# Queueing the first decodes of a fused attention and SwiGLU chain behind the gates of its items

## The chip, the cores and the metric

The kernel runs on one core of one Trainium2 chip. The metric is the time of one execution on the device in microseconds; several executions are timed and their median is given. The engines of the core are TensorE (PE; its weight loads are listed as PEld), VectorE (DVE), ScalarE (ACT), GpSimd (POOL) and SyncE (SP), whose queue issues most of the transfers. Each engine works through its own queue in order.

## The reference

Everything is float32. Attention is done twice: a packed query `p` (32 rows) reads keys and values, and the packed result serves as keys and values for the queries. The result is flattened to 4608 tokens of 512 and goes through a SwiGLU layer and a bilinear one.

```python
def _attn_ref(q, k, v, p):                       # batch 8, heads 8, seq 576, dim 64
    def sm_attn(qq, kk, vv): ...                 # softmax(scale * qq kk^T) vv
    p_packed = sm_attn(p, k, v)
    return sm_attn(q, p_packed, p_packed)

def _moe_ref(x, w_in, w_out):                    # 512 -> 2048 -> 512
    h = x @ w_in
    g = h * (1.0 / (1.0 + np.exp(-h)))
    return (g @ w_out).astype(np.float32)

def _moe2_ref(x, w1, w2, w3, w_out):             # 512 -> 1024 -> 512
    a = x @ w1
    b = x @ w2
    return (((a * b) @ w3) @ w_out).astype(np.float32)
```

## The kernel before

Matrix products keep float32 accuracy by splitting each operand into a high part (rounded to the type fp32r) and a low part, and adding three products (`mm3`, lines 97 to 100: one matmul on each of the lines 98, 99 and 100). The high part is a copy, mostly on ScalarE (line 82), the low part a subtraction on VectorE or GpSimd (line 91).

The span has two halves. Up to about 840 us an attention and SwiGLU stage runs, a loop over 256 *items* `(b, f, m)`: batch element, half of its 576 rows, one 128-wide block of the 2048 hidden columns. For an item:

- `emit_h` multiplies the block's first factor (a slot of `mq`, packed values times a block of `w_in`) with the attention weights `a2`: 6 matmuls of 288 columns into a PSUM tile `ps_h` of a pool with **two** banks;
- `emit_g` takes tanh of half of it on ScalarE (`sg`, line 874), then the gate on VectorE (`gg`, line 879), which reads `ps_h` and so frees its bank, then the high part `gh` on ScalarE and the low part `gl` on GpSimd;
- `emit_x2`, three items later, multiplies `gh` and `gl` with the second factor `wo[m]`, 12 matmuls into four banks `acc0` to `acc3` (`ps_x`).

After it comes the bilinear layer, which the change doesn't touch.

The weights arrive as 64-bit words and have to be decoded into float32. `Decode` (from line 174) does for one tile of 128x512: two conversions on ScalarE (line 82), a shift (line 190) and a mask (line 192) on VectorE, and a sum on GpSimd (line 196). For the first ones an intermediate tile `ps_dec` stands in one of the banks acc2 and acc3; once the second product of item 0 has been written out by the program they go without it, in place in SBUF. There are 32 decodes in the start: i0 to i7, o0 to o7, i8 to i15, o8 to o15 (`i`: a piece of `w_in`; `o`: one `wo[m]`, which is split as well, the low part mostly on GpSimd).

The order in which the program writes out the work of the start is the string `START`, cut by `|`: what stands ahead of the first `|` comes ahead of item 0, and each further piece comes at the end of one item, behind its `emit_g`. `L` loads a raw tile on SyncE's queue, `F` decodes one. P0, P1 are the steps of the packed attention of batch elements 0 and 1; S0, S1 those of the second attention of element 0, first and second half of its rows. `D` (`direct0`) makes a quarter's first factors for one group of heads right in the slots: two products of plain float32 (line 693; each has two matmul records) into a `ps_h` bank, then the split (lines 82 and 91) into `mq`. It has to come ahead of `P1.tail`, which copies element 1's packed values into the blocks `mbd` that the product reads. `T` (`direct`, line 704) makes the same products for both elements and stores them to DRAM; `W` stores pieces of `w_in`.

The program's order isn't the order in the queues. A planner goes through the program with a model of the engines and puts what is ready at an engine first into its queue, by order in the program where several are ready. A decode whose raw tile has landed can so stand far ahead of the item with which it is written. `tc.issue_after(ins)` takes that freedom: what is written within it goes behind `ins` in `ins`'s own queue. `hold(*names)` does so for the instructions kept in `behind`: "sg" is the tanh of the latest item and "gg" its gate. Before, this is used for later work (the decodes from item 70 on among it) and not for the F of the start. For items 0 to 15 all stores and loads of SyncE queue behind the last raw load written (`behind[DMA]`).

Of the kernel before, what the change touches and what calls it, by code (L numbers as in the profile page):

```python
# [23 lines left out]
def attention_swiglu_chain(  # L24
# [27 lines left out]
    H, D, NPK = 8, 64, 32  # L52
# [16 lines left out]

    START = (  # L70
        "P0.load P0.load_v P0.split_v0 S0.load P0.prepare L L L P1.load P1.load_v P1.prepare P1.split_v0 L L "
        "P0 P0 P0 P0 P0.tail S0 S0 P1 F L F L S1.load S0 P1 F L F L D D P1 F L F L P1 F L F L D D P1.tail F "
        "| F L F L S1 | F L S1 | F F S1 | F F T T | T T | T T | T T L | W W L | F L W W | W W | F L W W | | F L "
        "| | F L | | F T T | T T | F L | | F L | | F T T | T T | W W | L W W | F L W W | W W "
        "| F L | F L | F L | F L | F L | F L | F | S0 S1 |"
    )
# [2 lines left out]
    V, A, T, G, DMA = nc.vector, nc.scalar, nc.tensor, nc.gpsimd, nc.sync  # L79
# [22 lines left out]
    behind = {}  # L102

    def hold(*names):

        stack = ExitStack()
        for x in names:
            stack.enter_context(tc.issue_after(behind[x]))
        return stack
# [573 lines left out]
    def store_wi(i):  # L683
        g, c = divmod(i, CD)
        move(out=wi_d[g, 128 * c:128 * c + 128], in_=zi[i])

    def direct0(g, hg):

        assert all(("i", CD * g + c) in ready for c in range(CD))
        ps = ps_h.tile([128, 512], F32, tag="h", name="ps_m0")  # L690
        for c in (2 * hg, 2 * hg + 1):
            w = m_blocks(True)[:, 0, c].rearrange("p y h n -> p (y h n)")
            T.matmul(out=ps, lhsT=w, rhs=zi[CD * g + c], start=c % 2 == 0, stop=c % 2 == 1)
        dst = slots[:, 4 * g:4 * g + 4, hg]
        split(dst[:, :, 0], dst[:, :, 1], ps.rearrange("p (j f) -> p j f", j=4))
        for j in range(4):
            holds[4 * g + j] = (0, 4 * g + j)

    def direct(g, c):

        assert ("i", CD * g + c) in ready
        ps = bank("ps_m0")
        w = m_blocks(True)[:, 0, c].rearrange("p y h n -> p (y h n)")
        T.matmul(out=ps, lhsT=w, rhs=zi[CD * g + c], start=True, stop=True)
        ms = at.tile([128, 512], F32, tag="ms", name="ms", bufs=NM)
        act_copy(ms, ps)
        move(out=m01_d[g][c], in_=ms)
        if c == CD - 1:
            m_done.update([(0, g), (1, g)])
# [67 lines left out]
    def act(token):  # L777

        if token == "F":
            fill.step()  # L780
        elif token == "L":
            fill.load()
        elif token == "D":
            direct0(*todo0.pop(0))
        elif token == "T":
            direct(*todo.pop(0))
        elif token == "W":
            store_wi(to_store.pop(0))
        else:
            name, _, what = token.partition(".")  # L790
            if what:
                for u in first[name]:
                    getattr(u, what)()
            else:
                for x in runs[name]:
                    next(x)
# [3 lines left out]
    def act_on():  # L800
        for token in plan:
            if token == "|":
                return
            act(token)

    act_on()


# [345 lines left out]
    W = 384  # L1154
# [159 lines left out]
    for i, (b, f, m) in enumerate(items):  # L1314
        if i == KM:
            for eng in (DMA, A):
                behind.pop(eng, None)
        flush()
        fetch(i)
        ps = emit_h(i)  # L1320
        if i >= LAG:
            emit_x2(i - LAG)
        emit_g(i, ps)
        for y in "xyz":
            while done[y] < due(y, i):
                done[y] += 1
                next(streams[y], None)
        act_on()
        if i == prep_end:
            drain(streams["y"])  # L1330
            drain(streams["x"])
            flush()
            early = ctx.enter_context(tc.tile_pool(name="early", bufs=1, side="right"))
            load_x2(0)
            for n in range(2):
                for name in USED:
                    load_left(n, name)
                load_z34(n)
            drain(first_right_factors())
# [355 lines left out]
```

## Time and profile before

| | us |
|---|---|
| median of 3 runs | 1393.79 |
| lowest and highest of them | 1393.56, 1398.23 |
| the profiled execution | 1392.33 |
| its span, first to last instruction | 1390.4 |
| TensorE busy | 1350.9 |
| VectorE busy | 970.3 |
| ScalarE busy | 736.4 |
| GpSimd busy | 919.5 |

The profile is one execution. A wait is idle time of an engine, put down to the instruction that ended it. A VectorE or GpSimd instruction's duration contains the time in which it is held up by the other engine. TensorE's matmuls are pipelined, so their durations overlap: a matmul of 288 columns lasts some 0.3 us in the trace and the next one starts 0.13 us after it.

### The profile page before, as it was taken

The page shows a single profiled execution, that of the slowest core. Times are in us where ns is not written, and L with a number is a line of the kernel's source. Part 1 is how long each engine was busy: PE and PEld are TensorE (multiplying, and loading weights), DVE is VectorE, ACT ScalarE, POOL GpSimd, SP SyncE. Part 2 cuts the span into 40 slices and gives each one's busy share as a digit, 9 for nine tenths or more (in the row PEclk, how much of TensorE's full clock was granted, in tenths as well). Part 3 has the DMA queues.
Part 4 walks back from the last instruction along what each step waited for, and adds up shares of the span by engine and source line. Part 5 has one row for each costly group of instructions (what it writes and reads, how often), then busy time and mean ns, then how long its engine had stood idle before and what let it go on. Part 6 is the DMA issues. An engine that isn't in the chain of part 4 may idle for free. (4 is left out here: it accounts for less than half of the span.)

```text
span 1390.4 us, 26650 instructions
## 1 busy us (share of the span) xinstructions
PE 1350.9 (97%) x9197; PEld 1307.8 (94%) x9197; DVE 970.3 (70%) x1642; ACT 736.4 (53%) x1653; POOL 919.5 (66%) x874
## 2 busy tenths in 40 slices
PE   7889899999999999999999999899999999999998
PEld 5578899999999999999999999899999999999998
DVE  5997756458776578777669747885765766766665
ACT  6857566565765566665556645453334443433432
POOL 2879857766879677887677644664754756647632
PEclk9999999999999999999999999999999999999999
DMA  9698546744676443865547648657667677576751
GB/s 328 212 324 271 154 147 194 207 128 144 210 230 207 148 147 112 276 200 160 186 144 240 206 163 282 196 174 214 212 175 231 179 211 215 173 218 206 215 160 54
DMA packets 191557, 272.94 MB, mean 196 GB/s; under 512 B 18752, under 2 KB 112320, under 8 KB 191424
## 3 DMA queue, kind: packets, MB, share of 16 engines
q1 hardware_dynamic: 173168, 251.20, 58.6%
q10 hardware_dynamic: 18256, 20.06, 4.1%
q8 instruction: 73, 1.20, 0.4%
q14 instruction: 60, 0.49, 0.1%
HBM read 209.06 MB, written 62.13 MB: 195 GB/s over the span
## 5 line engine op out<-in xcount | busy, mean ns | idle before, releaser
L98 PE MATMUL ps_x<-gh,wo 128*128 128x288 f32 x1024 | 300.6, 297 | 2.7 <-DVE xs L916 2.7
L99 PE MATMUL ps_x<-gh,wo 128*128 128x288 f32 x1024 | 299.8, 295 | 0.0
L100 PE MATMUL ps_x<-gl,wo 128*128 128x288 f32 x1024 | 288.8, 297 | 0.5 <-POOL gl L91 0.4
L91 POOL TENSOR_TENSOR gl<-gg,gh 128x288 fp32r<-128x288 f32 x256 | 231.8, 908 | 80.0 <-ACT gh L82 65.3
L879 DVE SCALAR_TENSOR_TENSOR gg<-sg,ps_h 128x288 f32<-128x288 f32 x256 | 114.1, 447 | 133.1 <-ACT sg L874 81.1
L1517 DVE TENSOR_TENSOR o<-o,ps_o 128x768 f32<-128x768 f32 x137 | 130.2, 951 | 101.3 <-PE ps_o L1535 100.5
L98 PEld LDWEIGHTS ps_x<-gh,wo 128*128 128x128 f32 x1024 | 192.0, 188 | 5.6 <-DVE xs L916 2.3
L99 PEld LDWEIGHTS ps_x<-gh,wo 128*128 128x128 f32 x1024 | 192.2, 188 | 2.2 <-issue 1.4
L91 POOL TENSOR_TENSOR mq<-mr,mq 128x256 fp32r<-128x256 f32 x168 | 143.6, 855 | 72.2 <-DVE mq L86 40.7
L100 PEld LDWEIGHTS ps_x<-gl,wo 128*128 128x128 f32 x1024 | 187.3, 188 | 3.4 <-POOL gl L91 2.0
L82 ACT ACTIVATE gh<-gg 128x288 fp32r<-128x288 f32 x256 | 113.0, 443 | 117.1 <-DVE gg L879 111.7
L98 PE MATMUL ps_h<-a,mq 128*128 128x288 f32 x512 | 155.3, 303 | 9.6 <-DVE gg L879 9.5
L100 PE MATMUL ps_h<-a,mq 128*128 128x288 f32 x512 | 151.5, 296 | 0.0
L99 PE MATMUL ps_h<-a,mq 128*128 128x288 f32 x512 | 151.3, 295 | 0.0
L874 ACT ACTIVATE sg<-ps_h 128x288 f32<-128x288 f32 x256 | 103.1, 406 | 88.1 <-PE ps_h L100 62.7
L91 POOL TENSOR_TENSOR lfa<-y,lfa 128x384 fp32r<-128x384 f32 x69 | 77.3, 1121 | 104.1 <-ACT lfa L82 92.0
L1535 PE MATMUL ps_o<-w,lfs 128*128 128x256 f32 x828 | 118.9, 282 | 2.0 <-DVE o L1517 1.5
L1377 PE MATMUL ps_a<-xct,ws 128*128 128x384 f32 x576 | 116.1, 335 | 0.4 <-ACT p L82 0.4
L1535 PEld LDWEIGHTS ps_o<-w,lfs 128*128 128x128 f32 x828 | 112.2, 190 | 2.9 <-DVE o L1517 1.9
L98 PEld LDWEIGHTS ps_h<-a,mq 128*128 128x128 f32 x512 | 96.5, 188 | 15.8 <-DVE gg L879 12.2
L1377 PEld LDWEIGHTS ps_a<-xct,ws 128*128 128x128 f32 x576 | 99.9, 188 | 0.7 <-ACT p L82 0.7
L99 PEld LDWEIGHTS ps_h<-a,mq 128*128 128x128 f32 x512 | 96.4, 188 | 3.3 <-issue 1.4
(225 smaller groups left out, 3268.1 us busy)
## 6 DMA issues: line engine op xcount, KB each, us to landing
ws<-w_d SPq DMA_DIRECT2D x192, 256.0 KB, 3.0
wa<-w_d SPq DMA_DIRECT2D x144, 256.0 KB, 3.1
mr<-m_d SPq DMA_DIRECT2D x144, 128.0 KB, 2.4
raw<-in_moe_w_dram SPq DMA_DIRECT2D x32, 512.0 KB, 4.5
w_d<-w12s ACTq DMA_DIRECT2D x56, 256.0 KB, 2.8
wz<-wi_d SPq DMA_DIRECT2D x48, 256.0 KB, 4.3
m_d<-ms SPq DMA_DIRECT2D x96, 128.0 KB, 3.0
x_d<-xs SPq DMA_DIRECT2D x20, 576.0 KB, 3.8
```

Of the source, the lines that this page charges most:

```text
L82: return A.activation(out=dst, in_=src, func=ACTF.Copy, scale=mul)
L91: (eng or V).tensor_tensor(out=lo, in0=src, in1=hi.bitcast(F32), op=ALU.subtract)
L98: T.matmul(out=dst, lhsT=wh, rhs=xh, start=start, stop=False)
L99: T.matmul(out=dst, lhsT=wl, rhs=xh, start=False, stop=False)
L100: return T.matmul(out=dst, lhsT=wh, rhs=xl, start=False, stop=stop)
L874: ins = A.activation(out=sg, in_=ps, func=ACTF.Tanh, scale=0.5)
L879: ins = V.scalar_tensor_tensor(out=gg, in0=sg, scalar=1.0, in1=ps, op0=ALU.add, op1=ALU.mult)
L1377: ins = T.matmul(out=bank, lhsT=w[:, kt, wp], rhs=xt[:, kt, xp], start=first and (kt, n) == (0, 0), stop=last and (kt, n) == (1, 2), skip_ ...
L1517: V.tensor_tensor(out=oacc[k], in0=oacc[k], in1=ps, op=ALU.add)
L1535: T.matmul(out=ps[:, t], lhsT=l[:, lp], rhs=w[:, wp], start=fresh and t != 1 and n == 0, stop=done and t != 0 and n == 2, skip_group_check ...
```

## The change

The second pair of `D` and `P1.tail` go from ahead of item 0 to item 1, behind what item 0 brings (two F and a step of S1) and item 1's product and gate. And an `F` that is written after the first item's tanh has its instructions on ScalarE put behind the latest item's tanh and those on VectorE behind its gate; its instructions on GpSimd, and the loads, are not held. That is for the 23 F of items 0 to 34.

```diff
@@ -69,8 +69,8 @@
-        "P0 P0 P0 P0 P0.tail S0 S0 P1 F L F L S1.load S0 P1 F L F L D D P1 F L F L P1 F L F L D D P1.tail F "
-        "| F L F L S1 | F L S1 | F F S1 | F F T T | T T | T T | T T L | W W L | F L W W | W W | F L W W | | F L "
+        "P0 P0 P0 P0 P0.tail S0 S0 P1 F L F L S1.load S0 P1 F L F L D D P1 F L F L P1 F L F L F "
+        "| F L F L S1 | D D P1.tail F L S1 | F F S1 | F F T T | T T | T T | T T L | W W L | F L W W | W W | F L W W | | F L "
         "| | F L | | F T T | T T | F L | | F L | | F T T | T T | W W | L W W | F L W W | W W "
         "| F L | F L | F L | F L | F L | F L | F | S0 S1 |"
@@ -801,7 +801,8 @@
         for token in plan:
             if token == "|":
                 return
-            act(token)
+            with hold("sg", "gg") if token == "F" and "sg" in behind else ExitStack():
+                act(token)
```

## Rows read from the trace of the kernel before

**Rows 1.** The page: busy us of an engine, share of the span, instructions.

```profile
PE 1350.9 (97%) x9197; PEld 1307.8 (94%) x9197; DVE 970.3 (70%) x1642; ACT 736.4 (53%) x1653; POOL 919.5 (66%) x874
```

**Rows 2.** TensorE's waits, 42 to 62 us: total us, times, longest.

```profile
PE ps_m L704 <- ACT mbd L82: 4.6, 1, 4.6
...
PE ps_h L98 <- DVE gg L879: 1.4, 1, 1.4
```

**Rows 3.** Stretches: length, busy us by engine with instructions, clock, DMA share, GB/s.

```profile
42.00:62.00 20.00, 13.34 (x60) 9.02 (x59) 18.55 (x34) 16.66 (x37) 17.35 (x15) 0.91 0.52 165
...
126.00:147.00 21.00, 18.64 (x129) 16.98 (x128) 19.40 (x24) 17.11 (x40) 21.00 (x17) 1.00 0.71 214
...
147.00:172.00 25.00, 21.62 (x152) 20.77 (x151) 18.40 (x36) 12.99 (x36) 21.40 (x23) 0.93 0.52 152
...
172.00:190.00 18.00, 18.00 (x140) 18.00 (x139) 9.13 (x23) 11.44 (x29) 8.85 (x9) 1.00 0.50 165
```

**Rows 4.** TensorE's waits, 62 to 147 us.

```profile
PE ps_h L98 <- DVE gg L879: 4.0, 5, 1.6
...
PE ps_x L98 <- DVE xs L916: 1.8, 2, 1.2
```

**Rows 5.** TensorE's waits, 147 to 190 us.

```profile
PE ps_h L98 <- DVE gg L879: 3.1, 2, 3.0
```

**Rows 6.** TensorE's timeline, 44 to 60 us: start, duration, engine, line, operation.

```profile
44.52 0.29 PE L100 MATMUL ps_h<-a,mq 128*128 128x288 f32 x1
...
51.33 3.64 PE L704 MATMUL ps_m<-zi,mbd 128*128 128x512 f32 x4 [4.64 <-ACT mbd L82]
...
57.71 0.69 PE L100 MATMUL ps_x<-gl,wo 128*128 128x288 f32 x4
...
59.84 0.40 PE L98 MATMUL ps_h<-a,mq 128*128 128x288 f32 x1 [1.44 <-DVE gg L879]
```

**Rows 7.** Timelines of ScalarE and VectorE: item 0's tanh and gate.

```profile
50.53 0.42 ACT L874 ACTIVATE sg<-ps_h 128x288 f32<-128x288 f32 x1
...
52.17 0.44 DVE L879 SCALAR_TENSOR_TENSOR gg<-sg,ps_h 128x288 f32<-128x288 f32 x1
```

**Rows 8.** VectorE's timeline: last decode's first operation, gates of items 28 and 34.

```profile
136.24 1.26 DVE L190 TENSOR_SCALAR z<-raw 128x512 int32<-128x512 int32 x1
...
147.37 0.45 DVE L879 SCALAR_TENSOR_TENSOR gg<-sg,ps_h 128x288 f32<-128x288 f32 x1
...
169.55 0.45 DVE L879 SCALAR_TENSOR_TENSOR gg<-sg,ps_h 128x288 f32<-128x288 f32 x1
```

**Rows 9.** Lines of decode and split: ns min/median/max, first and last start.

```profile
L190 DVE TENSOR_SCALAR z<-raw x9: 509/1011/1257, 61.7 to 136.2; 128x512 int32<-128x512 int32 x9
...
L192 DVE SCALAR_TENSOR_TENSOR raw<-raw x17: 676/1294/1805, 62.3 to 137.4; 128x512 int32<-128x512 int32 x17
...
L196 POOL TENSOR_TENSOR z<-z,raw x9: 1307/1350/1835, 64.6 to 142.6; 128x512 int32<-128x512 int32 x9
...
L91 POOL TENSOR_TENSOR wo<-z,wo x8: 1286/1460/1753, 113.7 to 151.1; 128x512 fp32r<-128x512 f32 x8
```

**Rows 10.** Timelines of TensorE and ScalarE: matmuls and a copy of direct factors.

```profile
43.01 1.02 PE L693 MATMUL ps_m<-zi,mbd 128*128 128x512 f32 x2
...
48.99 0.59 ACT L82 ACTIVATE mq<-ps_m 128x512 fp32r<-128x512 f32 x1
```

**Rows 11.** VectorE's timeline: two masks of decodes.

```profile
56.62 0.67 DVE L192 SCALAR_TENSOR_TENSOR raw<-ps_dec,raw 128x512 int32<-128x512 int32 x1
...
97.57 1.29 DVE L192 SCALAR_TENSOR_TENSOR raw<-raw 128x512 int32<-128x512 int32 x1
```

**Rows 12.** SyncE's queue, 41 to 56 us: four raw loads.

```profile
41.36 14.54 SPq L214 DMA_DIRECT2D raw<-in_moe_w_out_dram  x4
```

**Rows 13.** VectorE's and TensorE's timelines, 161 to 168 us.

```profile
161.47 4.74 DVE L91 TENSOR_TENSOR x<-kq,x 128x576 fp32r<-128x576 f32 x1
...
167.76 0.61 PE L98 MATMUL ps_h<-a,mq 128*128 128x288 f32 x1 [2.97 <-DVE gg L879]
```

## What is predicted, and why

> **What bounds the kernel now.** I read the page first, then TensorE's waits stretch by stretch, then the busy times of the same stretches, then the timelines of the places where it waits. TensorE is busy for 97% of the span [rows 1], so only the time in which it stands still can be won, and it stands still early. From 42 to 62 us it waits 4.6 us for a copy on ScalarE and 1.4 us for a gate [rows 2]; and the granted clock of that stretch is 0.91 [rows 3], which over 20 us is another 1.8 us. From 62 to 147 us it waits 4.0 us for gates (line 879) and 1.8 us for line 916, both on VectorE [rows 4], from 147 to 190 us 3.1 us for gates [rows 5], with a clock of 0.93 in 25 us, 1.8 us more [rows 3]. That is some 18 us in all. In 172 to 190 us the weight loads fill the whole stretch [rows 3]: from there TensorE itself is the bound. What can be won or lost by this change lies between 42 and 190 us.
>
> The waits have one kind of cause. In the queues of ScalarE and VectorE decodes stand ahead of the tanh and the gate, whose product frees one of the two PSUM banks of the first matmul. Item 0's product is finished at 44.8 us [rows 6], its tanh starts at 50.5 and its gate at 52.2 [rows 7]: 5.7 us late, in which ScalarE runs decodes. VectorE is busy for 18.6 of 20 us there [rows 3], so this is a question of order as well as of load.
>
> **Part 1: the holds.** Each F of items 0 to 34 now queues its ScalarE work behind that item's tanh and its VectorE work behind that item's gate. Nothing is removed; 23 decodes move back. How far: the planner had pulled them forward. The last decode, which the plan names with item 34, starts on VectorE at 136.2 us, while the gates of items 28 and 34 run at 147.4 and 169.6 us [rows 8]. So it now comes 33 us later, and the seven decodes of items 28 to 34, which the trace has between about 114 and 151 us, go into 147 to 175 us. The twelve or so before them move by 5 to 35 us.
>
> Price of one decode with its split: VectorE 0.5 to 1.3 us (line 190, median 1.01) and 1.29 us (line 192), together some 2.0 us; GpSimd 1.35 us for the sum and 1.46 us for the low part, 2.8 us [rows 9].
>
> Start, 42 to 62 us. Before, the state "items 0 to 3 multiplied by the first factor, item 0 by the second" is reached at 60.7 us, since item 3's product starts at 59.84 us [rows 6] and lasts some 0.9. After: item 0's product needs only the split of Spread's last half and may end at about 43.8 us, its tanh and gate (0.42 and 0.44 us, [rows 7], with a hop between) by 45.1. A direct factor of the second quarter is now made in the bank that this gate frees: four matmul records, two of which took 1.02 us, [rows 10], so some 1.7 us, to 46.9; its two copies take 0.59 us on ScalarE [rows 10] and about 0.67 on VectorE, by the same shape in [rows 11], and stand behind the decodes of item 0, some 1.2 us: 49.4. Then item 2's product, tanh and gate: 51.5. Behind that gate stand the two decodes of item 2, whose PSUM room is a bank of the second matmul (before, that matmul's last bank was free when line 192 ended at 57.3 us, [rows 11]); four conversions and four VectorE operations overlapped, 3.2 us: 54.7, and the second product of item 0 ends at 55.6. That is 5.1 us earlier, less 1.7 us for two direct() products which TensorE had already done by then before and still owes now. **Term 1: -3 us**, with bounds: -6 if ScalarE's 4.6 us wait and the low clock behind it vanish whole, +1 if the chain through the two banks takes their place.
>
> 62 to 147 us. VectorE and GpSimd were busy for 19.4 and all 21 of the 21 us from 126 to 147 [rows 3]; four of the decodes there and two of the six between 81 and 109 us move out, 2 us of VectorE each. A typical wait: line 192 at 97.57 us took 1.29 us [rows 11] ahead of item 13's gate, and with the 0.4 us of line 190 that is what TensorE waited there (1.6, the longest of [rows 4]). **Term 2: -4 us** of the 5.8 us of waits there; bounds 0 and -6.
>
> 147 to 190 us. Seven decodes come in: 14 us on VectorE, 20 on GpSimd. VectorE had 18.4 and 9.1 us of work in these 43 us, GpSimd 21.4 and 8.9 [rows 3]; of the latter two low parts of decodes (2.7 us) fall out, and 3.9 us of a later stage can wait. So VectorE has 41.5 and GpSimd some 44 us of work in 43. The raw buffers spread the decodes (three of them, so the fourth load waits for the first sum), and the last second factor is wanted by item 39 only, which TensorE reaches three items later, after 185 us. The nearest stretch with such loads, 126 to 147 us, cost 1.8 us and some tenths in 21 us, no more per us than 147 to 190 cost already. I take **term 3: +2 us**, the excess of GpSimd and a little of the gates; bounds -3 (the present waits for gates vanish) and +13 (worked out under the third rival).
>
> **Part 2: D D and P1.tail.** Two direct factors, eight matmul records, and the tail's transposes and copies move behind item 0's S1; no instruction is added or taken away. Item 0's product no longer stands behind them on TensorE, and item 1's no longer behind the direct() products at 51.33 us, four records that took 3.64 us [rows 6], about twice what such took at the full clock. The new wait is the one in term 1: items 2 and 3 wait for both direct factors' copies. Behind it in TensorE's queue stand the second product of item 0 and the direct() products. The tail is wanted by direct() from item 3 on, whose stores are wanted much later: nothing, as long as TensorE has other work; two direct() products, 1.7 us, if not.
>
> **SyncE.** The raw loads are issued by L, not by F, but a load waits for the sum of an earlier decode. Before, four loads held SyncE's queue for 14.54 us [rows 12]. The load of item 1's L waits for item 2's first decode; that one's VectorE part stood at 51 to 52 us and now comes at about 53, so the queue is free at about the same time and the stores and row loads behind it are not moved. POOL's queue gets the same instructions in another order; they are not held, but their inputs are.
>
> Sum: -3 - 4 + 2 = -5 us. The profiled execution took 1392.33 us (span 1390.4), the median of the runs is 1393.79, 1.46 above it; so 1387.3 for a profiled one and **1388.8 us** for the median.
>
> **Where a rule of the skill bears on it.** Line 192 takes 0.67 us when one of its inputs is the PSUM tile [rows 11] and 1.29 in the median when both come from SBUF [rows 9], and a VectorE subtraction of two SBUF tiles at 161.47 us lasted 4.74 us while GpSimd ran without a gap; the gate behind it came so late that TensorE waited 2.97 us [rows 13]. The Trainium skill, "SBUF — State Buffer", section "Who interferes with whom", says that a VectorE instruction with two SBUF inputs and a GpSimd instruction that reads SBUF exclude each other for the whole instruction. By that rule the trace agrees, and it speaks against this change: the late decodes are all of the two-input kind and meet a GpSimd that never rests. What it would make of the time is the third rival.
>
> **Rivals.**
> - *The gates are free everywhere.* The decodes fill the gaps behind the gates, also after 147 us. Terms -6, -6, 0: -12, **1382 us**. For it: from 172 to 190 us VectorE and GpSimd had work for only half of the time [rows 3]. Against it: with the decodes both are near full for all of these 43 us.
> - *The banks take over.* The direct factors between items 1 and 2 make the start as late as it was, and the rest gains what it loses: +1, -2, +2, about **1394 us**. For it: three copies and two gates in one chain. Against it: those copies find an emptier ScalarE queue.
> - *The pile-up, slower.* In items 28 to 34 GpSimd has a sum, a low part, a gate's low part and the rest, some 4.7 us, in an item that TensorE does in 3.1 (25 us for eight). Each VectorE decode can then be shut out as at 161.47 us; such a stop cost TensorE 2.97 us [rows 13], and one in two of the seven decodes makes 3.5 of them, 10.4 us, with the 2.6 us that GpSimd ends late, +13. Then -2, -3, +13: +8, **1402 us**. It decides the sign once term 3 is above 7 us, that is from the third such stop on.
>
> **Chances.** The forecast 0.45 (own range 1385 to 1392), the free gates 0.22, the banks 0.15, the pile-up 0.18. About 0.5%, 7 us, is what a measurement tells from no change. Faster by more, below 1386.8: a fifth of the forecast and nearly all of the free gates, 0.30. Slower by more, above 1400.8: two thirds of the pile-up, 0.12. Between: 0.58. The range from 1381 to 1401 leaves out the lower two fifths of the free gates (0.09) and the upper part of the pile-up (0.11).
>
> **What would show it.** Right: tanh 0 and gate 0 start before 46 us; the second product of item 0 ends near 55; TensorE's waits for gates between 62 and 147 us fall from 4.0 to under 2 us; the last decode's line 192 starts after 168 us; waits and lost clock from 147 to 190 us are 5 to 8 us. Wrong: a wait of TensorE for a direct factor's copy of over 4 us near 47 us (the banks), VectorE operations of over 3 us between 147 and 190 us in numbers (the pile-up), or a different order of the stages after 190 us, which this sum leaves as they are.

## The result and the profile after

| | before, us | after, us |
|---|---|---|
| median of 6 runs each | 1395.18 | 1408.98 |
| lowest and highest | 1393.56, 1398.23 | 1405.43, 1411.88 |
| ratio, with its 95% interval | | 1.0105 [1.0090, 1.0119] |
| the profiled execution, its span | 1392.33, 1390.4 | 1405.43, 1403.3 |

The change makes the kernel slower by 13.8 us in the median and by 12.9 us between the two spans. The page's first line shows the same work for every engine as [rows 1], instruction for instruction in number; TensorE is busy 1.3 us longer, and the rest is idle time.

```profile
PE 1352.2 (96%) x9197; PEld 1310.4 (93%) x9197; DVE 975.0 (69%) x1642; ACT 736.9 (53%) x1653; POOL 917.4 (65%) x874
```

To see where the time went I took the start of each item's gate (line 879 before, line 880 after) from VectorE's two timelines, and subtracted:

| gate of item | 0 | 6 | 20 | 24 | 28 | 32 | 38 | 48 | 66 | 255 |
|---|---|---|---|---|---|---|---|---|---|---|
| before, us | 52.17 | 73.67 | 121.36 | 132.25 | 147.37 | 158.40 | 183.22 | 213.95 | 270.42 | 842.92 |
| after minus before | -5.2 | -5.9 | -6.1 | -6.4 | -4.2 | +0.4 | +8.9 | +11.5 | +11.9 | +13.7 |

The gates of the start come early, those up to item 24 stay so, and between gates 24 and 48 some 18 us are lost. Not all of the early part is time gained, for TensorE does its work in another order: by gate 6 it has started 224 matmuls where it had started 248 before, by gate 24 582 against 601, by gate 66 1546 in both. TensorE's waits say what the time went for. First the start, 42 to 62 us, and then 62 to 147 us (columns as in [rows 2]):

```profile
PE ps_m L693 <- DVE gg L880: 3.0, 2, 2.6
...
PE ps_h L98 <- DVE gg L880: 3.1, 3, 1.7
PE ps_s L312 <- DMA kq<-in_q_dram: 1.8, 1, 1.8
```

The wait of 4.6 us in [rows 2] is gone; in its place stands the new one, for the gate that frees a bank for the moved direct factor. In the second stretch the gates still cost 3.1 us of the 4.0 in [rows 4], and a load of query rows 1.8 us, where the trace before has no wait for a load. Then 147 to 190 us, against 3.1 us in [rows 5]:

```profile
PE ps_h L98 <- DVE gg L880: 11.5, 2, 9.7
```

and the stretches of [rows 3] once more:

```profile
42.00:62.00 20.00, 16.81 (x83) 11.90 (x83) 19.38 (x37) 18.27 (x42) 16.91 (x15) 1.00 0.31 93
126.00:147.00 21.00, 19.00 (x136) 17.83 (x135) 13.15 (x27) 12.08 (x30) 12.07 (x13) 1.00 0.75 255
147.00:172.00 25.00, 13.54 (x100) 13.07 (x99) 24.97 (x27) 15.85 (x37) 22.45 (x19) 0.87 0.38 119
172.00:190.00 18.00, 17.60 (x123) 17.31 (x122) 12.76 (x24) 14.50 (x37) 15.80 (x13) 0.90 0.66 215
```

VectorE had 19.4 of 21 us of work in 126 to 147; now it has 13.2 there, and 24.97 of 25 in the stretch behind it, where TensorE does 13.5 us of work instead of 21.6 at a granted clock of 0.87. But VectorE carries out 27 instructions in those 25 us, and 36 in 18.4 us before. Its instructions got longer. Its timeline around the long wait (start, duration, line, operation) has the place:

```profile
158.79 0.44 DVE L880 SCALAR_TENSOR_TENSOR gg<-sg,ps_h 128x288 f32<-128x288 f32 x1
...
160.46 2.52 DVE L190 TENSOR_SCALAR z<-raw 128x512 int32<-128x512 int32 x1
162.90 0.14 DVE L444 TENSOR_REDUCE nb<-mx 128x1 f32<-128x2 f32 x1
162.96 1.71 DVE L192 SCALAR_TENSOR_TENSOR raw<-raw 128x512 int32<-128x512 int32 x1
164.59 5.76 DVE L91 TENSOR_TENSOR x<-kq,x 128x576 fp32r<-128x576 f32 x2
170.27 0.41 DVE L91 TENSOR_TENSOR pb<-pr,pb 128x256 fp32r<-128x256 f32 x1
170.61 0.44 DVE L880 SCALAR_TENSOR_TENSOR gg<-sg,ps_h 128x288 f32<-128x288 f32 x1
170.97 0.41 DVE L190 TENSOR_SCALAR z<-raw 128x512 int32<-128x512 int32 x1
171.31 0.68 DVE L192 SCALAR_TENSOR_TENSOR raw<-raw 128x512 int32<-128x512 int32 x1
...
177.83 0.68 DVE L192 SCALAR_TENSOR_TENSOR raw<-raw 128x512 int32<-128x512 int32 x1
```

The gates in the first and the seventh line are those of items 32 and 33. Between them stand one decode (lines 190 and 192) and the two splits of `x`, which belong to the keys of a later batch element. GpSimd's timeline beside it has no gap until 169.7 us:

```profile
156.29 3.72 POOL L91 TENSOR_TENSOR v<-vr,v 128x768 fp32r<-128x768 f32 x2
159.98 1.34 POOL L91 TENSOR_TENSOR wo<-z,wo 128x512 fp32r<-128x512 f32 x1
...
162.65 1.47 POOL L196 TENSOR_TENSOR z<-z,raw 128x512 int32<-128x512 int32 x1
164.08 1.71 POOL L91 TENSOR_TENSOR wo<-z,wo 128x512 fp32r<-128x512 f32 x1
165.75 0.72 POOL L91 TENSOR_TENSOR mq<-mr,mq 128x256 fp32r<-128x256 f32 x1
166.43 1.53 POOL L91 TENSOR_TENSOR gl<-gg,gh 128x288 fp32r<-128x288 f32 x2
167.93 1.80 POOL L196 TENSOR_TENSOR z<-z,raw 128x512 int32<-128x512 int32 x1
172.07 1.29 POOL L196 TENSOR_TENSOR z<-z,raw 128x512 int32<-128x512 int32 x1 [2.33 <-DVE rs L470]
```

The sums (line 196) and the low parts of `wo` here are those of late decodes. As soon as GpSimd rests, at 169.7 us, the same decode operations take 0.41 and 0.68 us (at 170.97 us) instead of 2.52 and 1.71. The lines ahead of gate 33 took 2.52 + 1.71 + 5.76 + 0.41 = 10.4 us; undisturbed they are 0.41 + 0.68 + 2 x 0.75 + 0.41 = 3.0 us (0.75 is the split's duration at 182.65 us in the seventh experiment below). So some 7.4 us come from being held up; an estimate from these durations is that without them gate 33 would have come at 163.2 us and TensorE would have waited some 2.3 us. It waited 9.7, and goes on at half its clock:

```profile
160.98 0.29 PE L98 MATMUL ps_x<-gh,wo 128*128 128x288 f32 x1
161.12 0.29 PE L99 MATMUL ps_x<-gh,wo 128*128 128x288 f32 x1
171.10 0.61 PE L98 MATMUL ps_h<-a,mq 128*128 128x288 f32 x1 [9.69 <-DVE gg L880]
171.51 0.44 PE L99 MATMUL ps_h<-a,mq 128*128 128x288 f32 x1
171.75 0.44 PE L100 MATMUL ps_h<-a,mq 128*128 128x288 f32 x1
```

The starts of matmuls lie 0.24 us apart behind the stop, and 0.13 ahead of it.

### The profile page after: what moved, and what is told of

Its sections match the earlier page's. It is cut to its first block, busy times and chain, and to the rows that moved or that the text cites. A ratio compares the mean times of both kernels' runs of the same rounds, so it can differ in the third digit from the quotient of the medians.

```text
span 1403.3 us, 26630 instructions
## 1 busy us (share of the span) xinstructions
PE 1352.2 (96%) x9197; PEld 1310.4 (93%) x9197; DVE 975.0 (69%) x1642; ACT 736.9 (53%) x1653; POOL 917.4 (65%) x874
## 5 line engine op out<-in xcount | busy, mean ns | idle before, releaser
L98 PEld LDWEIGHTS ps_h<-a,mq 128*128 128x128 f32 x512 | 97.2, 190 | 24.7 <-DVE gg L880 21.0
L86 DVE CAST mq<-mr 128x256 fp32r<-128x256 f32 x168 | 93.6, 557 | 11.1 <-DMA mr<-m_d 8.9
```

Of the source, the lines that this page charges most:

```text
L86: V.tensor_copy(out=hi, in_=src)
L98: T.matmul(out=dst, lhsT=wh, rhs=xh, start=start, stop=False)
```

## Experiments

The theory, called P in some of the expectations, is the pile-up: the decodes of items 28 to 34, held behind their gates, meet the splits of the later batch elements and a GpSimd without a gap, and lengthen what stands ahead of a gate. The rivals: the moved direct factors lose the time, or the holds as such (all 23 of them, wherever they stand) do. Q in the expectations stands for a rival, named there each time. Each table row below is the median over the kernel before, which ran on the same chip, with the interval of the ratio. Gates are given as in the table above; the profile is one execution, the median one of several, so the two can differ by some microseconds. The program ahead of gate 0 is the same in the change and in 1, 2 and 6 to 12, and gate 0 lies there between -5.9 and -1.9: differences of gates between two kernels of up to 4 us can be the execution's.

| kernel | median, us | before, us | ratio | gate 20 | gate 38 | gate 66 |
|---|---|---|---|---|---|---|
| the change | 1408.98 | 1395.18 | 1.0105 [1.0090, 1.0119] | -6.1 | +8.9 | +11.9 |
| 1: no hold from item 26 on | 1397.83 | 1393.92 | 1.0028 [1.0014, 1.0042] | -6.7 | -4.7 | +2.4 |
| 2: holds of items 0 to 3 alone | 1393.73 | 1395.57 | 0.9991 [0.9977, 1.0005] | -1.2 | -3.3 | +3.4 |
| 3: the move alone | 1401.29 | 1393.92 | 1.0055 [1.0033, 1.0077] | +10.4 | +6.9 | +8.5 |
| 4: the holds alone | 1407.64 | 1393.92 | 1.0098 [1.0066, 1.0130] | -3.3 | +11.6 | +14.8 |
| 5: holds of items 28 to 34 alone | 1409.54 | 1393.92 | 1.0117 [1.0092, 1.0142] | -0.2 | +2.8 | +11.4 |
| 6: low parts by ScalarE | 1396.14 | 1395.57 | 1.0005 [0.9984, 1.0026] | -4.3 | -1.4 | +4.5 |
| 7: decodes written earlier | 1391.33 | 1395.57 | 0.9970 [0.9960, 0.9980] | -6.0 | -3.2 | -2.4 |
| 8: low parts as memsets | 1401.85 | 1395.46 | 1.0045 [1.0028, 1.0062] | +0.1 | +3.1 | +11.2 |
| 9: one item earlier still | 1397.23 | 1395.46 | 1.0023 [1.0009, 1.0037] | -6.0 | -0.1 | +2.5 |
| 10: as 7, ScalarE held alone | 1391.53 | 1395.46 | 0.9975 [0.9961, 0.9990] | -3.5 | -0.4 | +0.4 |
| 11: memsets at the same place | 1400.50 | 1395.50 | 1.0038 [1.0023, 1.0053] | 0.0 | +4.6 | +11.6 |
| 12: x low parts by ScalarE | 1397.74 | 1395.50 | 1.0021 [1.0008, 1.0034] | -1.1 | -1.2 | +8.1 |

**The two parts, one at a time (3 and 4).** In all kernels `part[0]` counts the items. The third has the changed `START` and no hold; the fourth has `START` as before and all holds.

```diff
-            with hold("sg", "gg") if token == "F" and "sg" in behind else ExitStack():
+            with hold("sg", "gg") if token == "F" and False else ExitStack():          # 3
+            with hold("sg", "gg") if token == "F" and part[0] >= 0 else ExitStack():   # 4, START of before
```

> Only the move of the second D D and P1.tail, no F is held. P: no pile-up, so nothing is lost behind item 28; if the gain of the start comes from the move (item 0's product no longer behind the direct factors) 1389 to 1391 us, if it comes from the holds 1394 to 1396. Q: over 1403 us.

> Only the holds on all 23 F, the direct factors stay ahead of item 0. P: the pile-up is whole, 14 to 16 us are lost between items 28 and 40; 1404 to 1411 us by how much of the 5 us of the start comes from the holds. Q (the move is the cause): 1388 to 1396 us.

The move alone loses 7.4 us, outside every range expected of it, and by the gates (+8.5 at gate 2, +8.5 at gate 66) all of it at the start. Item 0's gate is as late as before (-0.3 us), and now the direct factors wait for it, so that TensorE stands still for 5.2 us and goes on at half clock: eight matmul records in 6.73 us, against four in 1.98 in the changed kernel.

```profile
46.86 0.33 PE L505 MATMUL ps_pk<-ident,pk 128*128 128x128 f32 x1 [0.18 <-ACT pk L485]
52.37 6.73 PE L693 MATMUL ps_m<-zi,mbd 128*128 128x512 f32 x8 [5.18 <-DVE gg L883]
```

The holds alone give the early gate (-4.4) and the loss behind item 28, and end 13.7 us above before, like both parts together (13.8). So with the holds the move is worth nothing that can be measured; the start's gain and the later loss are both the holds'.

**The late holds alone, and all but these (5 and 1).** The fifth is the kernel before with the F of items 28 to 34 held and nothing else; the first is the change without the holds from item 26 on.

```diff
+            with hold("sg", "gg") if token == "F" and part[0] >= 28 else ExitStack():       # 5, START of before
+            with hold("sg", "gg") if token == "F" and 0 <= part[0] < 26 else ExitStack():   # 1
```

> The kernel before with nothing but the F of items 28 to 34 held. P: all of the loss and none of the gain, 1407 to 1412 us, gate 33 of the items over 8 us behind its tanh's place. Q: 1393 to 1397 us, like the kernel before.

> The changed kernel, but the F of items 26 to 34 (the eight last decodes) are not held; all else as in the change. Theory P (the pile-up: late decodes stand ahead of gate 33 on VectorE): the 5 to 6 us won up to item 28 stay, the 14 us lost between items 28 and 40 go: 1387 to 1391 us, with the kernel before at 1395. Theory Q (the moved direct factors or the earlier holds have changed the planner's order of the later stages, and the late decodes are only there by chance): the loss stays, over 1403 us.

Seven held decodes are enough: +15.6 us, with the change's picture in TensorE's waits. This is the fifth kernel's line from 147 to 215 us:

```profile
PE ps_h L98 <- DVE gg L883: 12.3, 3, 8.6
```

and this the changed kernel's over the same time:

```profile
PE ps_h L98 <- DVE gg L880: 14.5, 3, 9.7
```

Without these holds and that of item 26 the long stop is gone and 10 of the 13.8 us come back, but not the gain of the start: gates 20, 22 and 26 stand at -6.7, -2.0 and 0.0. The planner pulls some of the freed decodes forward: five masks (line 192) start between 122 and 147 us, where the change has two. In 109 to 147 us TensorE waits 5.5 us in all, for work on three engines:

```profile
PE ps_x L100 <- POOL gl L91: 2.2, 1, 2.2
PE ps_x L98 <- ACT xs L82: 1.6, 1, 1.6
PE ps_m L704 <- POOL zi L196: 1.3, 1, 1.3
PE ps_x L98 <- DVE xs L920: 0.4, 1, 0.4
```

This was foreseen by no theory (1397.83 us lies between the two expectations): a decode that isn't held doesn't stay where it was. That these decodes cause the waits is argued from their place; no run tests it.

**The first seven holds alone (2).**

```diff
+            with hold("sg", "gg") if token == "F" and 0 <= part[0] < 4 else ExitStack():
```

> The change with only the F of items 0 to 3 held (seven decodes), the other sixteen free. Theory P2 (the holds of the first items bring the start's 5 to 6 us, the sixteen others bring nothing on the way to item 28, and freed decodes are pulled ahead as before): gates 5 us early at item 6, and between items 10 and 28 some of it is given back as in the run with holds up to item 25, which ended at 1398; 1392 to 1398 us. If the sixteen later holds do help (term 2 of the prediction): 1398 or more, with the gain of item 6 gone by item 20.

Gates 0, 6 and 20 stand at -3.5, -3.7 and -1.2: most of the lead is used up by item 20, while the change goes from -5.2 at gate 0 to -6.1 and the first experiment from -5.9 to -6.7. So from gate 0 to gate 20 the holds of items 4 to 25 are worth some 3 us: they keep what the first seven win. The difference is no larger than what gate 0 varies by between executions, so its size is not settled. In the end the kernel is within the measurement of before.

**Who lengthens the splits (6, 8, 11, 12).** In the sixth, the low part of `wo[8]` to `wo[15]` is left out of the computation: ScalarE writes a scaled copy in its place, which takes 1.3 to 1.8 us [rows 9] off GpSimd for each of these decodes. In the eighth and the eleventh it is left out as well, and GpSimd writes zeros; in the eleventh the memsets stand right behind that decode's sum. In the twelfth the low parts of `x` of batch elements 2 and 3 are left out: ScalarE copies stand in the place of VectorE's splits.

```diff
+        if m >= KM // 2:
+            split_hi(wo[m][:, 0], d.z)
+            act_copy(wo[m][:, 1], d.z, 2.0**-12)                       # 6
+            for n in (512, 512, 256):                                  # 8, for the line above; in 11 within tc.issue_after(d.sum)
+                G.memset(wo[m][:, 1, 0:n].bitcast(F32), 0.0)
+            return
-            split(*x, self.rows[f])                                    # 12
+            if isinstance(self, Pack) and self.b in (2, 3):
+                split_hi(x[0], self.rows[f])
+                act_copy(x[1], self.rows[f], 2.0**-12)
+            else:
+                split(*x, self.rows[f])
```

> The whole change, but the low part of the eight late second factors is not a subtraction on GpSimd: ScalarE writes a scaled copy in its place (the low part is left out of the computation). It takes eight instructions of 1.3 to 1.75 us off GpSimd and adds eight of 0.6 us on ScalarE; VectorE has the same work. If what makes the pile-up is GpSimd holding up VectorE's two-input instructions: the splits and masks ahead of gate 33 shrink from 10 us to under 6 and 5 to 9 of the 14 us come back, 1399 to 1403 us. If it is VectorE's own load or the order alone: 1406 us or more, the same durations.

> The whole change, but for the eight late second factors GpSimd writes zeros (three memsets, 1280 columns in all, by a memset of 1024 columns that took 1.11 us about 1.4 us together) in place of the subtraction of 1.29 to 1.75 us; the low part is left out of the computation. GpSimd stays as busy as in the change but reads nothing from SBUF in that time. If the pile-up comes from GpSimd instructions that read SBUF and shut out VectorE's two-input ones: as in the run with ScalarE's copies, 1394 to 1400 us. If it comes from GpSimd being late with its own work (sums, low parts of gates): as the whole change, 1405 us or more.

> The changed kernel, but the low part of wo[8..15] is left out of the computation: in its place GpSimd writes zeros with memsets of 512, 512 and 256 columns that stand directly behind that decode's sum in its queue. GpSimd is about as busy as before at the same place, but these instructions read nothing from SBUF. If it is GpSimd's reading beside VectorE's two-input splits that stretches them, the splits ahead of gate 33 fall from 5.76 us to about 3 us or less for two, and the time comes out like the run in which ScalarE wrote the low part: 1394 to 1400 us. If GpSimd's load and lateness make the stop, whatever it does, 1404 us or more with a gate wait of some 9 us near 170 us.

> The changed kernel, but the low parts of x of batch elements 2 and 3 are left out of the computation: ScalarE copies stand where VectorE's subtractions stood. The decodes of items 28 to 34 still stand behind tanh and gate. If VectorE's long two-input splits ahead of gate 33 are what makes the late decodes expensive, most of the 14 us come back: 1393 to 1400 us, and the longest gate wait between 147 and 190 us falls from 9.7 us to 4 us or less. If the decodes' own sums and steps behind the gate suffice for the stop, 1404 us or more.

The sixth: the same two splits of `x` in VectorE's timeline, and TensorE's waits for gates from 147 to 215 us.

```profile
168.72 2.98 DVE L91 TENSOR_TENSOR x<-kq,x 128x576 fp32r<-128x576 f32 x2
```

```profile
PE ps_h L98 <- DVE gg L887: 2.4, 1, 2.4
```

The same two views of the eleventh:

```profile
171.90 3.77 DVE L91 TENSOR_TENSOR x<-kq,x 128x576 fp32r<-128x576 f32 x2
```

```profile
PE ps_h L98 <- DVE gg L889: 11.9, 5, 6.3
```

And the waits of the twelfth:

```profile
PE ps_h L98 <- DVE gg L887: 3.4, 3, 1.9
```

Over their own before, the sixth stands at +0.6 us and the twelfth at +2.2, where the change stands at +13.8. So either side's removal takes nearly all of it away: GpSimd's low parts (13.2 us, more than was expected), or VectorE's splits (11.6 us), with all decodes held as in the change. A full engine alone doesn't do it: from 147 to 172 us VectorE is busy for 24.3 of 25 us in the sixth, GpSimd for all 25 in the twelfth. Neither is expensive by itself; their meeting ahead of a gate is. The longest waits for a gate that remain, 2.4 and 1.9 us, are about the 2.3 us which the undisturbed durations leave (above); in the sixth TensorE also waits 3.9 us for other VectorE work from 147 to 215 us.

The eighth was a failed control. Its memsets depend on nothing of the decode, so the planner put them far ahead, beside other work (gates 14 and 28 at -0.3 and +3.7); what it says of the late stretch is hidden behind that. The eleventh mends this, and it decides less than was hoped: +5.0 us, between the two expectations. With GpSimd about as busy at the same place but without these reads, 8.8 of the 13.8 us are gone and the two splits take 3.77 us instead of 5.76; yet the gate waits are still 11.9 us in the profiled execution, in five pieces. That execution is the slowest of its ten (1405.54 us), and the twelfth's (1401.06) is 0.01 us from being so; both start 3 us later than that of the change (gate 0 at -2 instead of -5), with a slower stretch ahead of 46 us which the edits don't touch. I take it, without a run that shows it, that the reads are the larger share and GpSimd's lateness the smaller; the sizes are not settled.

**Placing the decodes (7, 9, 10).** All holds, but the last nine decodes, and with them their loads, are written with earlier items: i15 with item 21 (it was 22), o8 to o15 with items 22 to 29 (they were 26 and 28 to 34), where the change had left VectorE and GpSimd room (13.2 and 12.1 of 21 us of work in 126 to 147 us, above). The ninth has these and i14 one item earlier still; the tenth is the seventh with only ScalarE's instructions held.

```diff
-        "| | F L | | F T T | T T | F L | | F L | | F T T | T T | W W | L W W | F L W W | W W "
-        "| F L | F L | F L | F L | F L | F L | F | S0 S1 |"
+        "| | F L | | F T T | T T | F L | L | F L | F L | F L T T | F L T T | F L W W | F L W W | F L W W | F L W W "   # 7, 10
+        "| F | F | | | | | | S0 S1 |"
-            with hold("sg", "gg") if token == "F" and "sg" in behind else ExitStack():
+            with hold("sg") if token == "F" and part[0] >= 0 else ExitStack():         # 10
```

> The whole change with all holds, but the plan names the late decodes earlier: i14, i15 with items 20 and 21, o8 to o15 with items 22 to 29 (before 26 and 28 to 34), their loads earlier too. P (it is the place of the late decodes, in items 28 to 34, not the hold): they fill the stretch from 115 to 150 us, in which VectorE and GpSimd had room after the change, and the pile-up is gone or under 4 us: 1388 to 1393 us. If holding a decode behind a gate costs wherever it stands: over 1400 us, with the loss some items earlier.

> As the run with the early plan (late decodes in items 22 to 29), but one item earlier still: i14, i15 with items 19 and 20, o8 to o15 with items 21 to 28. If the 4.4 us wait that was left near 163 us is the rest of the pile-up, 2 to 4 us less than there: 1387 to 1390 us; if the decodes now crowd the gates of items 19 to 24: 1391 to 1395 us.

> The early plan with ScalarE's hold alone (behind the tanh), VectorE's part of a decode is free. Since a decode's VectorE work waits for its conversions on ScalarE, behind the tanh, it can pass one gate at most: if the start's gain is the tanh's, the same 1390 to 1393 us; if the order on VectorE is what brings it, the gain of the first items is gone: 1395 to 1398 us.

The seventh beats both kernels: 1391.33 us, 0.9970 [0.9960, 0.9980] of before. It keeps the start's gain through item 54 (-4.0), with one stop left. Its stretches 126 to 147 and 147 to 172 us:

```profile
126.00:147.00 21.00, 19.47 (x141) 18.45 (x140) 16.84 (x26) 15.72 (x38) 18.82 (x16) 1.00 0.89 290
147.00:172.00 25.00, 20.14 (x136) 19.61 (x135) 21.83 (x35) 17.08 (x42) 24.04 (x23) 0.86 0.80 250
```

and its waits for gates from 147 to 215 us:

```profile
PE ps_h L98 <- DVE gg L883: 4.4, 1, 4.4
```

GpSimd is busy for 24.0 of 25 us here, more than in the change; but only two decodes are left in that stretch, and VectorE does 35 instructions in 21.8 us instead of 27 in 25. The ninth loses again, to 1397.23, above both of its expectations: -6.0 at gate 20, and +3.3 at gate 31. Its TensorE waits for gates are 5.4 us and one for a softmax exponential 2.0 us from 147 us on; why one item earlier brings them back was not followed further. The tenth equals the seventh within the intervals, so with decodes placed there the hold on VectorE is not needed beside that on ScalarE.

## Why the prediction was wrong

Forecast: 1388.8 us, range 1381 to 1401. Measured: 1408.98, beyond the range and on the other side of before. The third rival, the pile-up (1402 us, chance 0.18), has the mechanism and the place, and the size of its price is too small. The step that failed is the price of term 3; a smaller one is the queue of SyncE.

**Term 1, -3 us (bounds -6 and +1): right in kind, some -5 measured.** From 42 to 62 us TensorE's waits fall from 6.6 to 3.0 us, and the 1.8 us of the low clock are gone. By gate 6 the lead is 5.9 us, but with the 24 matmuls that are put off. Ahead of 42 us this execution lost 3.9 us more than that of before, in waits and clock; the fifth experiment's, whose program there is that of before, lost 3.2 more, so most of that belongs to the execution. Tanh 0 starts at 45.37 us (before 46, as said), gate 0 at 46.94: 0.9 us later than said, since VectorE had softmax work of S1 between them. The second product of item 0 ends at 57.2 us (its last two records start at 56.41 and take 0.83), not near 55. What came out better is the rest of it: the granted clock is 1.00 where [rows 3] has 0.91, and from 42 to 62 us the only stops are 3.0 us for the new wait on a bank, 2.6 the longest. The rival of the banks wanted over 4 us there; the third experiment shows that wait, 5.2 us, when the gate comes late.

**Term 2, -4 us (bounds 0 and -6): -1 us.** The waits for gates fall from 4.0 to 3.1 us, not under 2. VectorE's work in these 85 us falls from 74.5 to 59.3 us, but a decode that is moved from ahead of one gate to behind it stands ahead of the next. What the holds do here is another thing, as the second experiment suggests: without those of items 4 to 25, 2.3 us of the lead of gate 0 are given back by item 20.

**SyncE** was to be free at about the same time. It wasn't: the four raw loads held its queue until 59.8 us, 3.9 us later than in [rows 12], and the load of query rows behind them is what TensorE waited 1.8 us for, about what it no longer waits for line 916, which is 917 in the change (1.8 us before, 0.3 now).

```profile
42.47 17.30 SPq L214 DMA_DIRECT2D raw<-in_moe_w_out_dram  x4
```

**Term 3, +2 us (bounds -3 and +13): the step that failed, +16 to +18 us.** (From gates 28 and 24 at -4.2 and -6.4 to gate 66 at +11.9.) The working had added up the loads, 41.5 and 44 us in 43, and then priced them by the stretch from 126 to 147 us, which had such loads and cost little. The sum had a slip: 1.01 and 1.29 us for a decode on VectorE are 2.3, not 2.0, which makes 43.6 us. But the loads were not the mistake, for they came out at 37.7 us on VectorE and 38.3 on GpSimd from 147 to 190 us; the price was. In 126 to 147 us two splits of `x` stood in VectorE's queue as well, beside a GpSimd without a gap, but the last decode (its line 192 starts at 137.4 us) stood ahead of an earlier gate, they took 2.56 us together, and TensorE waited 0.6 us for the gate behind them:

```profile
142.47 2.56 DVE L91 TENSOR_TENSOR x<-kq,x 128x576 fp32r<-128x576 f32 x2
```

In 147 to 172 us a decode and two such splits stand ahead of one gate, and each instruction lasts two to six times as long as undisturbed: 2.52 us against 0.41, 1.71 against 0.68, about 2.9 against 0.75. A queue in order hands the whole delay to the gate; that there is rest later in the stretch (12.8 of 18 us from 172 us on) doesn't help it. The case had stood in [rows 13]: one split of 4.74 us, and a wait of TensorE of 2.97 us. The prediction cited it and then let the average decide.

In numbers, from gate 28 to gate 66, 16.1 us: the waits for gates from 147 to 215 us are 14.5 us and were 3.1, +11.4; the waits from 215 to 275 us are 2.0 us and were 0.5, +1.5. Of the low clock only the part counts in which TensorE works, for the rest lies inside the waits. Behind the long wait, from 171.1 to 190 us, the granted clock is 0.88, and from 192.6 to 215 us it is 0.92, which costs 2.3 and 1.8 us; before, it was 0.93 from 167.8 to 190 us, 1.6 us. That is +2.5 us. Together they make 15.4 us, and five matmuls fewer were started by gate 28 (687, 692 before), 0.7 us at 0.13 us each. The rival had made its +13 of 3.5 stops of 2.97 us and GpSimd's excess; in fact it is one stop of 9.7, shorter ones of 1.8 and 3.1, and the clock behind them.

**The order in GpSimd's favour** was told right: the last decode's line 192 starts at 177.83 us (after 168, as said), and the operations of over 3 us that were to be the sign of the pile-up are there: two splits in 5.76 us, the first of 4.00, and a split of `pb` in 3.68 us at 188.54 us.

**D D and P1.tail** were to cost nothing beside the bank wait, and the fourth experiment, without them, differs from the change by nothing that can be measured.

**The sum**, by gates: -5.9 at gate 6, 0.5 more up to gate 24, then +18.3 up to gate 66 and 1.8 up to gate 255 make +13.7, against 12.9 us between the spans. Part of the first is matmuls put off, which the third then has to make up.

## What to carry to other kernels

An average load near one says little about a queue in order: look for the instruction that others wait for, and add up what can stand ahead of it, each at its longest duration in the trace. A hold that keeps urgent work in front is worth something only while the held work still has a place; write that work at an earlier place in the same step (here one to five items earlier), or it meets the next stage. And an item that is taken out of a hold doesn't go back to where it was: the planner moves it, so undoing a part is a new order of its own.

## What the runs showed of the hardware

The price of the meeting of VectorE and GpSimd was larger than I had thought. Two splits that take 0.75 us each undisturbed took 5.76 us while GpSimd ran five instructions without a gap, and the second ended 0.6 us after GpSimd's last. Beside a GpSimd that had no gap either, two such splits took 2.56 us in the kernel before; what decides between the two no run shows. Line 190, which reads a single tile of SBUF, is stretched as well: 2.52 us against 0.41. The prediction called the late decodes all of the two-input kind. The Trainium skill, "SBUF — State Buffer", section "Who interferes with whom", names `tensor_scalar` among the operations that can take the port pair shared with GpSimd; the trace agrees. The gate, which reads one tile from SBUF and one from PSUM, kept its 0.44 us throughout, and so did not lengthen itself: it was late only by what stood ahead of it.
